# Low parts of the gate and value weights and the scaling of the output weights, on GpSimd instead of VectorE

## The chip, the cores and the metric

The kernel runs on one core of a Trainium2 chip. The metric is device time in microseconds (us). The core has five engines with a queue of instructions each: TensorE (PE; its weight loads are shown as PEld), VectorE (DVE), ScalarE (ACT), GpSimd (POOL) and SyncE (SP, which here issues DMAs). An engine takes its instructions in order; semaphores make it wait for others.

## The reference

Three layers, one after the other, in 32-bit floats (weights come as 64-bit words):

```python
scores = (q @ k.T) / sqrt(64)                  # 4 batches, 8 heads, 576 rows, 64 wide
attn = softmax(where(scores >= max(scores) - tau, scores, -1e9))
x = (attn @ v)  ->  2304 tokens x 512          # heads side by side
xn = x / rms(x) * rms_g                        # first MLP: 512 -> 1536 -> 512
g = xn @ w_gate
y = (silu(g) * (xn @ w_val)) @ w_out
P = exp(y @ gate - max); 8 x (rows and columns of P scaled)
out = sum over 8 experts e of P[:, e] * (relu(y @ w1[e]) @ w2[e])   # 512 -> 1024 -> 512
```

## The kernel before

A 32-bit operand goes through TensorE as two 16-bit parts: a high part (the value rounded) and a low part (the value minus the high part). A product is then three matmuls: high by high, high by low, low by high.

**Attention** runs over batches b, chunks c of 128 rows and heads h; a tile (b,c,h) is 128 x 576 scores. PE makes S (line 290), VectorE its maximum (300), ScalarE the exponent e (304), VectorE the mask (306), ScalarE the high part hl (311), GpSimd the low part in two pieces (312, 313), a transposing DMA makes eT (315), and PE multiplies with v into pv (338), three tiles behind S. After the eight heads of a chunk, `end_main` scales a row of tokens and makes xnT. Chunk 4 of a batch holds the 64 rows that are left and has four tiles of two heads.

**The first MLP** goes over nine pairs j of token blocks: `mlp_in(j)` makes gv (line 538) for 12 slices f of the hidden width, and `mlp_out(j)` 72 matmuls into x2 (572). The first pair needs the weights: `prep_group(gi)` calls `prep_in` for a third of the columns of the gate and of the value weights. There 64-bit words are loaded and turned into floats (lines 440 to 444) in the space of the output weights (`stage`, three places, the names `raw` and `wo`), a scale is found from their norms (465 to 470), ScalarE writes the high part (473), and the low part is made (474). `prep_out` converts the 12 slices of the output weights (also lines 440 to 444, with squares in line 498), finds a scale over all of them, and then for each slice scales it into one of two buffers r (515), makes the high part on ScalarE (516) and the low part on GpSimd (517).

The code is written in the order of the data, but a scheduler orders each engine's instructions by a timeline of its own, with attention given priority; so an operation on another engine moves others too, on all engines. Only the last stage, the experts, from about 790 us on, has an order of PE written out by hand (line 1148). This core of `prep_out` is what the change touches besides line 474:

```python
rr = pw.tile([P, 4, HD], F32, tag="x2", name="wof")
for f in range(KF):
    r = rr[:, f % 2 * 2 : f % 2 * 2 + 2].rearrange("p o d -> p (o d)")
    V.tensor_scalar(r, wo32[:, f], sf[:, f // n : f // n + 1], None, ALU.mult)
    A.activation(wo[:, f, 0, :], r, AF.Copy)
    G.tensor_tensor(wo[:, f, 1, :], r, wo[:, f, 0, :], ALU.subtract)
```

Of the kernel before, what the change touches and what calls it, by code (L numbers as in the profile page):

```python
# [12 lines left out]
ALU = mybir.AluOpType  # L13
# [6 lines left out]
def kernel(  # L20
# [24 lines left out]
    V, A, G, T = nc.vector, nc.scalar, nc.gpsimd, nc.tensor  # L45
# [371 lines left out]
    wo32 = wo.rearrange("p k l f -> p k (l f)").bitcast(F32)  # L417
# [33 lines left out]
    def prep_in(src, w, gi, name):  # L451

        bits = src.bitcast(I32)
        raw = stage[:, staged[0] % 3]
        staged[0] += 1
        ps = psx.tile([P, DM], F32, tag="mx", name=f"{name}n{gi}", bufs=1)
        cols = slice(gi * DM, (gi + 1) * DM)
        for kk in range(KD):
            wd = words(
                bits[kk * P : (kk + 1) * P, 2 * gi * DM : 2 * (gi + 1) * DM], f"{name}w{gi}_{kk}"  # L460
            )
            to_f32(raw[:, kk], wd, f"{name}l{gi}_{kk}")
            sq = pw.tile([P, 2 * P], F32, tag="u", name=f"{name}q{gi}_{kk}", bufs=2).bitcast(BF16)
            A.activation(sq, raw[:, kk], AF.Square)
            T.matmul(ps, lhsT=gsq[:, kk : kk + 1].to_broadcast([P, P]), rhs=sq, start=kk == 0, stop=kk == KD - 1)
        n2 = small([P, 1], name + "n2", bufs=2)
        V.tensor_reduce(n2, ps, AX.X, ALU.max)
        s, inv = norm_scale(n2, 1, 9, f"{name}{gi}")
        gs = small([P, KD], f"{name}gs{gi}")
        V.tensor_scalar(gs, g_sb, s[:, 0:1], None, ALU.mult)  # L470
        for kk in range(KD):
            sk, hi = gs[:, kk : kk + 1], w[:, 0, kk, cols]
            A.activation(hi, raw[:, kk], AF.Copy, scale=sk)
            V.scalar_tensor_tensor(w[:, 1, kk, cols], raw[:, kk], sk, hi, ALU.mult, ALU.subtract)
        return inv

    g32 = []
# [12 lines left out]
    def prep_out():  # L490

        bits = moe_w_out.bitcast(I32)
        n = KF // NG
        om = small([P, KF], "om")
        for f in range(KF):
            wd = words(bits[f * P : (f + 1) * P, :], f"wo{f}", ("x2", "x2t")[f % 2])
            sq = to_f32(wo32[:, f], wd, f"wol{f}").bitcast(BF16)[:, 0:DM]
            A.activation(sq, wo32[:, f], AF.Square, accum_out=om[:, f : f + 1])
        for _ in range(2):
            V.tensor_tensor(  # L500
                om.rearrange("p (g f) -> p g f", g=NG),
                om.rearrange("p (g f) -> p g f", g=NG),
                igv.to_broadcast([P, NG, n]),
                ALU.mult,
            )
        om1 = small([P, 1], "om1")
        V.tensor_reduce(om1, om, AX.X, ALU.max)
        s, inv = norm_scale(all_max(om1, "womx"), 1, 9, "wout")
        V.tensor_scalar(ixs, inv, 2.0**10, None, ALU.mult)
        sf = small([P, NG], "wosf")  # L510
        V.tensor_scalar(sf, igv, s[:, 0:1], None, ALU.mult)
        rr = pw.tile([P, 4, HD], F32, tag="x2", name="wof")
        for f in range(KF):
            r = rr[:, f % 2 * 2 : f % 2 * 2 + 2].rearrange("p o d -> p (o d)")
            V.tensor_scalar(r, wo32[:, f], sf[:, f // n : f // n + 1], None, ALU.mult)
            A.activation(wo[:, f, 0, :], r, AF.Copy)  # L516
            G.tensor_tensor(wo[:, f, 1, :], r, wo[:, f, 0, :], ALU.subtract)

# [163 lines left out]
    for t in range(len(row) + LAG):  # L682
        before = tc.cur_priority
        with attention_order():
            if t < len(row):
                b, c, heads, n, g = row[t]
# [461 lines left out]
    with tc.manual_schedule(engines={mybir.EngineType.PE}):  # L1148
        for k, (c, j) in enumerate(ahead):
            u, f = c // 2, c % 2  # L1150
# [85 lines left out]
```

## Time and profile before

| | |
|---|---|
| time, median of 3 runs | 2144.69 us (2141.03 to 2146.65) |
| the profiled execution's own time | 2142.97 us |
| its span, first to last instruction | 2141.2 us |
| busy in the span: PE | 1958.7 us (91%) |
| VectorE | 1628.3 us (76%) |
| ScalarE | 1307.4 us (61%) |
| GpSimd | 1358.6 us (63%) |

A share is a mean over stages with different limits: attention with the preparation of the weights first, then attention with the first MLP, then the experts. The span is some 2 us shorter than the execution's own time, which has the start and the end around it.

### The profile page before, as it was taken

What the parts mean: (1) busy time and instruction counts of PE and PEld (TensorE: products, weight loads), DVE (VectorE), ACT (ScalarE), POOL (GpSimd) and SP (SyncE); (2) the same over time, 40 slices, a digit from 0 to 9 for tenths busy, and PEclk for the clock granted to TensorE, in tenths of its full rate; (3) what the DMA queues carried; (4) which work ended last, traced back from release to release, by engine and by line L of the source; (5) the groups of instructions that cost most, each with busy time, mean ns of one, the idle gap of its engine ahead of it and who ended that gap; (6) DMA issues with size and microseconds to landing.
All of it is one profiled execution on the core that took longest, in us unless ns stands there. A gap on an engine that the chain in (4) does not pass through costs nothing.

```text
span 2141.2 us, 43769 instructions
## 1 busy us (share of the span) xinstructions
PE 1958.7 (91%) x16462; PEld 1454.1 (68%) x16462; DVE 1628.3 (76%) x3408; ACT 1307.4 (61%) x2804; POOL 1358.6 (63%) x1404
## 2 busy tenths in 40 slices
PE   1458788899999899899999999999999999999999
PEld 0236556677776667677777777777777777777777
DVE  6898677778753345897888888888888888888866
ACT  5887777878752247656655555555556555555552
POOL 1346546567652347666777777677777777777754
PEclk9769999999999999999999999999999999999999
DMA  9977679877854818244343334334434443433332
GB/s 269 209 170 151 137 138 163 178 133 144 143 90 128 191 55 227 94 136 124 118 141 121 120 124 136 118 116 141 123 118 134 125 124 124 143 119 121 104 99 81
DMA packets 373669, 290.46 MB, mean 136 GB/s; under 512 B 286160, under 2 KB 299600, under 8 KB 373456
## 3 DMA queue, kind: packets, MB, share of 16 engines
q1 hardware_dynamic: 372864, 287.64, 51.8%
q8 instruction: 129, 2.11, 0.4%
q14 instruction: 84, 0.69, 0.1%
q0 software_dynamic: 64, 0.00, 0.0%
q10 hardware_dynamic: 528, 0.02, 0.0%
HBM read 195.71 MB, written 21.23 MB: 101 GB/s over the span
## 4 chain that ended last, share of the span: by engine, by line
PE 64%; DVE 2%; DMA 2%; SPq 2%; ACT 0%; issue 0%; POOL 0%; DVEq 0%; ACTq 0%; POOLq 0%
PE P L1090 30%; PE X L1022 17%; PE Z L1022 12%; PE gv L538 3%; PE x L572 2%; SPq L833 1%; DMA xo<-x2d 1%; DVE w L733 1%; DMA xs<-x2d 1%; SPq L837 0%; DVE acc L1104 0%; DMA x2d<-xs 0%; DMA eT<-hl 0%; PE pv L338 0%; PE logits L875 0%
## 5 line engine op out<-in xcount | busy, mean ns | idle before, releaser
L1090 PE MATMUL P<-w,h 128*128 128x256 f16 x6048 | 768.6, 273 | 12.7 <-DVE w1mx L133 7.6
L1090 PEld LDWEIGHTS <-h 128*128 128x128 f16 x6048 | 591.9, 98 | 151.5 <-issue 16.2
L1022 PEld LDWEIGHTS <-w 128*128 128x128 f16 x4032 | 394.9, 98 | 194.1 <-issue 3.4
L1100 DVE SCALAR_TENSOR_TENSOR acc<-P,coef,acc 128x256 f32<-128x256 f32 x882 | 412.7, 477 | 100.8 <-PE P L1090 89.7
L1022 PE MATMUL X<-xo,w 128*128 128x384 f16 x2304 | 438.2, 327 | 1.3 <-ACT u2b L1042 0.9
L1022 PE MATMUL Z<-xo,w 128*128 128x384 f16 x1728 | 327.9, 326 | 0.0
L312 POOL TENSOR_TENSOR hl<-e,hl 128x512 f16<-128x512 f32 x144 | 173.9, 1207 | 210.4 <-ACT hl L311 136.1
L538 PE MATMUL gv<-xnT,wg 128*128 128x256 f16 x1296 | 171.7, 281 | 18.6 <-DVE u L548 17.6
L538 PE MATMUL gv<-xnT,wv 128*128 128x256 f16 x1296 | 169.1, 279 | 0.0
L538 PEld LDWEIGHTS <-wg 128*128 128x128 f16 x1296 | 127.6, 101 | 40.7 <-issue 21.1
L572 PE MATMUL x<-wo,tT 128*128 128x512 f16 x648 | 147.3, 382 | 6.8 <-ACT wo L516 3.7
L338 PE MATMUL pv<-vs,eT 128*128 128x64 f16 (+1 forms) x2240 | 102.2, 201 | 46.9 <-DMA eT<-hl 42.5
L338 PEld LDWEIGHTS <-eT 128*128 128x128 f16 (+1 forms) x2240 | 91.2, 106 | 76.9 <-DMA eT<-hl 61.2
L538 PEld LDWEIGHTS <-wv 128*128 128x128 f16 x1296 | 128.7, 100 | 18.1 <-issue 0.4
L300 DVE TENSOR_REDUCE nt<-S 128x1 f32<-128x576 f32 x144 | 107.1, 750 | 40.8 <-PE S L290 40.5
L306 DVE SCALAR_TENSOR_TENSOR e<-S,nt,e 128x576 f32<-128x576 f32 x144 | 116.5, 810 | 23.2 <-ACT e L304 22.8
L290 PE MATMUL S<-kT,qT 128*128 128x288 f16 (+1 forms) x320 | 65.6, 312 | 66.1 <-DVE e L306 35.6
L553 POOL TENSOR_TENSOR tT<-u,tT 128x256 f16<-128x256 f32 x108 | 74.9, 694 | 73.0 <-ACT tT L552 72.9
L572 PEld LDWEIGHTS <-tT 128*128 128x128 f16 x648 | 62.9, 98 | 81.6 <-issue 12.5
L304 ACT ACTIVATE e<-S,nt,c 128x576 f32<-128x576 f32 x144 | 117.5, 818 | 0.2 <-issue 0.2
L311 ACT ACTIVATE hl<-e 128x576 f16<-128x576 f32 x144 | 97.0, 676 | 24.9 <-DMA eT<-hl 13.7
L547 DVE SCALAR_TENSOR_TENSOR u<-u,gv 128x256 f32<-128x256 f32 x108 | 44.8, 415 | 73.7 <-ACT u L546 72.9
(2539 smaller groups left out, 3669.8 us busy)
## 6 DMA issues: line engine op xcount, KB each, us to landing
xo<-x2s SPq DMA_DIRECT2D x319, 384.0 KB, 3.1
w1r<-in_moe_w_dram SPq DMA_DIRECT2D x17, 1024.0 KB, 5.0
w2r<-in_moe_w_dram SPq DMA_DIRECT2D x17, 1024.0 KB, 6.6
x2s<-xo SPq DMA_DIRECT2D x17, 384.0 KB, 2.8
wgatew<-in_moe_w_gate_dram SPq DMA_DIRECT2D x12, 512.0 KB, 5.5
wo<-in_moe_w_out_dram SPq DMA_DIRECT2D x12, 512.0 KB, 4.1
wvalw<-in_moe_w_val_dram SPq DMA_DIRECT2D x12, 512.0 KB, 4.2
x2d<-xs SPq DMA_DIRECT2D x24, 256.0 KB, 2.6
```

The lines of the kernel that those rows point to most:

```text
L300: V.tensor_reduce(mx, sv, AX.XY, ALU.max)
L304: A.activation(ev, sv, AF.Exp, bias=nt[:, 0:1], scale=st["c2"][:, c : c + 1])
L306: V.scalar_tensor_tensor(ev, sv, nt[:, 1:2], ev, ALU.is_ge, ALU.mult, accum_out=sums[:, slot : slot + 1])
L311: A.activation(hl[:, 0:S], e, AF.Copy)
L312: G.tensor_tensor(hl[:, S + REM :], e[:, 0 : NCH * P], hl[:, 0 : NCH * P], ALU.subtract)
L338: T.matmul(o, lhsT=a, rhs=r, start=n == 0, stop=n == len(mm) - 1)
L538: T.matmul(gv[:, a, :], lhsT=w[:, l, kk, f * P : (f + 1) * P], rhs=xt[:, r * KD + kk, :], start=n == 0, stop=n == 3 * KD - 1,)
L553: G.tensor_tensor(t[:, 1, :], u, t[:, 0, :], ALU.subtract)
L572: T.matmul(ps, lhsT=tT[f][:, l, o : o + P], rhs=wo[:, f, r, :], start=n == 0, stop=n == 3 * KF - 1,)
L1022: T.matmul(ps, lhsT=w[:, a, l, kk, f * P : (f + 1) * P], rhs=xb[:, r * 2 + kk, :], start=n == 0 and j in (0, 1, 3), stop=n == 5, skip_grou ...
L1090: T.matmul(ps, lhsT=hs[u, ao, f][:, l, jj * P : (jj + 1) * P], rhs=w2[h][:, bo, r, f, :], start=n == 0 and j in (0, 1, 3), stop=n == 5, sk ...
L1100: main[True] = V.scalar_tensor_tensor(y, ps, coef[h][:, i : i + 1], y, ALU.mult, ALU.add)
```

## The change

```diff
@@ prep_in @@
             A.activation(hi, raw[:, kk], AF.Copy, scale=sk)
-            V.scalar_tensor_tensor(w[:, 1, kk, cols], raw[:, kk], sk, hi, ALU.mult, ALU.subtract)
+            G.tensor_scalar(raw[:, kk], raw[:, kk], sk, None, ALU.mult)
+            G.tensor_tensor(w[:, 1, kk, cols], raw[:, kk], hi, ALU.subtract)
@@ prep_out @@
-            V.tensor_scalar(r, wo32[:, f], sf[:, f // n : f // n + 1], None, ALU.mult)
+            G.tensor_scalar(r, wo32[:, f], sf[:, f // n : f // n + 1], None, ALU.mult)
```

The low part of a gate or value weight (24 of 128 x 512) was one operation of VectorE: raw times its scale, minus the high part. Now GpSimd scales raw in place, after ScalarE has read it, and then subtracts. The scaling of an output weight's slice (12 of 128 x 512) goes from VectorE to GpSimd as it is. Lines behind 474 have numbers greater by one in the changed kernel.

The scheduler's order changes with it. On GpSimd, at the first gate weights (wgategs is their scale, wg and wv the gate and value weights, hl the low parts of attention tiles), there stood in the kernel before:

```order
L312 TENSOR_TENSOR hl0_0_6_407<-e0_0_6_403,hl0_0_6_407 128x512
L313 TENSOR_TENSOR hl0_0_6_407<-e0_0_6_403,hl0_0_6_407 128x64
L312 TENSOR_TENSOR hl0_0_7_439<-e0_0_7_435,hl0_0_7_439 128x512
L313 TENSOR_TENSOR hl0_0_7_439<-e0_0_7_435,hl0_0_7_439 128x64
L312 TENSOR_TENSOR hl0_1_0_472<-e0_1_0_468,hl0_1_0_472 128x512
L313 TENSOR_TENSOR hl0_1_0_472<-e0_1_0_468,hl0_1_0_472 128x64
L312 TENSOR_TENSOR hl0_1_1_504<-e0_1_1_500,hl0_1_1_504 128x512
L313 TENSOR_TENSOR hl0_1_1_504<-e0_1_1_500,hl0_1_1_504 128x64
L312 TENSOR_TENSOR hl0_1_2_544<-e0_1_2_540,hl0_1_2_544 128x512
L313 TENSOR_TENSOR hl0_1_2_544<-e0_1_2_540,hl0_1_2_544 128x64
L358 TENSOR_TENSOR rs0_574<-ms0_572,mhalf_58 128x1
```

and in the changed one:

```order
L474 TENSOR_SCALAR wo_104<-wo_104,wgategs0_917 128x512 x4
L475 TENSOR_TENSOR wg_102<-wo_104,wg_102 128x512 x2
L312 TENSOR_TENSOR hl0_0_6_407<-e0_0_6_403,hl0_0_6_407 128x512
L313 TENSOR_TENSOR hl0_0_6_407<-e0_0_6_403,hl0_0_6_407 128x64
L475 TENSOR_TENSOR wg_102<-wo_104,wg_102 128x512 x2
L312 TENSOR_TENSOR hl0_0_7_439<-e0_0_7_435,hl0_0_7_439 128x512
L313 TENSOR_TENSOR hl0_0_7_439<-e0_0_7_435,hl0_0_7_439 128x64
L474 TENSOR_SCALAR wo_104<-wo_104,wvalgs0_981 128x512 x4
L312 TENSOR_TENSOR hl0_1_0_472<-e0_1_0_468,hl0_1_0_472 128x512
L313 TENSOR_TENSOR hl0_1_0_472<-e0_1_0_468,hl0_1_0_472 128x64
L475 TENSOR_TENSOR wv_103<-wo_104,wv_103 128x512 x3
```

So the scalings and subtractions of the weights stand between the low parts of attention tiles, the four scalings of a group mostly in one piece. On the whole 24 scalings and 21 subtractions stand ahead of the end of tile (0,2,3) there.

On PE, at the end of batch 0 (pv0_4 are the last products with v of batch 0, x2_0 and x2_1 the output products of the first MLP, line 572), there stood before:

```order
L338 MATMUL pv0_4_3075<-vs0_0_229,eT0_4_0_2435 64x64
L338 LDWEIGHTS eT0_4_0_2435
L338 MATMUL pv0_4_3075<-vs0_0_229,eT0_4_0_2435 64x64
L572 LDWEIGHTS tT0_0_1265
L572 MATMUL x2_0_1763<-wo_104,tT0_0_1265 128x512
L572 LDWEIGHTS tT0_0_1265
L572 MATMUL x2_1_1809<-wo_104,tT0_0_1265 128x512
L572 LDWEIGHTS tT0_0_1265
L572 MATMUL x2_0_1763<-wo_104,tT0_0_1265 128x512
```

and now, behind the last hidden slice gv0_11:

```order
L539 MATMUL gv0_11_1604<-xnT0_579,wv_103 128x256
L290 LDWEIGHTS qT1_0_2478
L290 MATMUL S1_0_0_3129<-kT1_0_2217,qT1_0_2478 128x288
L290 LDWEIGHTS qT1_0_2478
L290 MATMUL S1_0_1_3178<-kT1_0_2217,qT1_0_2478 128x288
L290 LDWEIGHTS qT1_0_2478
L290 MATMUL S1_0_0_3129<-kT1_0_2217,qT1_0_2478 128x288
L290 LDWEIGHTS qT1_0_2478
L290 MATMUL S1_0_1_3178<-kT1_0_2217,qT1_0_2478 128x288
L539 LDWEIGHTS wv_103
L539 MATMUL gv0_11_1604<-xnT0_579,wv_103 128x256
L539 LDWEIGHTS wv_103
```

Before, 62 of the 72 output products stand ahead of the first S of batch 1; now S of its first two tiles stands ahead of all 72, and the rest of the 72 stand among tiles up to (1,1,2).

On GpSimd, at the same place (wof is the scaled output weight, line 516 the moved scaling), there stands now:

```order
L516 TENSOR_SCALAR wof_1750<-wo_104,wosf_1748 128x512
L554 TENSOR_TENSOR tT0_8_1539<-u0_11_1629,tT0_8_1539 128x256
L516 TENSOR_SCALAR wof_1750<-wo_104,wosf_1748 128x512
L518 TENSOR_TENSOR wo_104<-wof_1750,wo_104 128x512
L312 TENSOR_TENSOR hl1_0_0_3141<-e1_0_0_3137,hl1_0_0_3141 128x512
L313 TENSOR_TENSOR hl1_0_0_3141<-e1_0_0_3137,hl1_0_0_3141 128x64
L516 TENSOR_SCALAR wof_1750<-wo_104,wosf_1748 128x512
L312 TENSOR_TENSOR hl1_0_1_3190<-e1_0_1_3186,hl1_0_1_3190 128x512
L313 TENSOR_TENSOR hl1_0_1_3190<-e1_0_1_3186,hl1_0_1_3190 128x64
L518 TENSOR_TENSOR wo_104<-wof_1750,wo_104 128x512
L516 TENSOR_SCALAR wof_1750<-wo_104,wosf_1748 128x512
L518 TENSOR_TENSOR wo_104<-wof_1750,wo_104 128x512
```

Before, the twelve subtractions of line 517 stood there in two runs of 2 and 10 with nothing of batch 1 between them; now scalings and subtractions stand among its first tiles, the last behind tile (1,0,5).

## Rows read from the trace of the kernel before

**Rows 1.** The page: busy tenths in 40 slices of 53.5 us.
```profile
PE   1458788899999899899999999999999999999999
...
DVE  6898677778753345897888888888888888888866
...
POOL 1346546567652347666777777677777777777754
```

**Rows 2.** The page: chain that ended last, by engine.
```profile
PE 64%; DVE 2%; DMA 2%; SPq 2%; ACT 0%; issue 0%; POOL 0%; DVEq 0%; ACTq 0%; POOLq 0%
```

**Rows 3.** Windows: busy us of each engine in four stretches.
```profile
core 0: us, PE busy (x) PEld busy (x) DVE busy (x) ACT busy (x) POOL busy (x), PEclk, DMA share, GB/s
67.90:143.80 75.90, 36.39 (x340) 22.00 (x339) 69.82 (x159) 63.59 (x131) 29.38 (x30) 0.63 0.79 183
143.80:237.03 93.23, 73.30 (x710) 51.02 (x708) 81.39 (x192) 71.54 (x167) 51.31 (x59) 0.92 0.68 142
240.00:420.00 180.00, 156.18 (x1681) 117.96 (x1681) 132.00 (x324) 142.65 (x330) 102.76 (x141) 0.96 0.81 155
420.00:640.00 220.00, 208.60 (x2376) 161.14 (x2375) 157.41 (x361) 163.30 (x376) 145.70 (x196) 1.00 0.74 133
```

**Rows 4.** Groups of VectorE by form, 67.9 to 143.8 us.
```profile
L474 DVE SCALAR_TENSOR_TENSOR wg<-wo,wgategs,wg 128x512 f16<-128x512 f32 x12 | 9.5, 819 | 0.0
L474 DVE SCALAR_TENSOR_TENSOR wv<-wo,wvalgs,wv 128x512 f16<-128x512 f32 x8 | 6.2, 780 | 0.0
```

**Rows 5.** Groups of GpSimd by form, 67.9 to 143.8 us.
```profile
L312 POOL TENSOR_TENSOR hl<-e,hl 128x512 f16<-128x512 f32 x14 | 19.4, 1382 | 42.0 <-ACT hl L311 29.0 <-issue 13.0
L313 POOL TENSOR_TENSOR hl<-e,hl 128x64 f16<-128x64 f32 x14 | 9.2, 655 | 0.0
```

**Rows 6.** Lines by source, whole span: durations ns min/median/max, first and last start.
```profile
L312 POOL TENSOR_TENSOR hl<-e,hl x144: 1143/1157/2405, 47.3 to 619.8; 128x512 f16<-128x512 f32 x144
...
L313 POOL TENSOR_TENSOR hl<-e,hl x144: 295/306/1552, 48.5 to 620.9; 128x64 f16<-128x64 f32 x144
```

**Rows 7.** Lines by source, whole span: two-input operations of equal shape.
```profile
L474 DVE SCALAR_TENSOR_TENSOR wg<-wo,wgategs,wg x12: 735/742/1634, 69.7 to 138.6; 128x512 f16<-128x512 f32 x12
...
L733 DVE SCALAR_TENSOR_TENSOR w<-w1s,w_s,w x48: 744/1203/1477, 754.0 to 1998.0; 128x512 f16<-128x512 f32 x48
...
L798 POOL TENSOR_TENSOR w1s<-w1r,w1s x16: 1266/1588/1710, 702.1 to 1980.3; 128x512 f32<-128x512 f32 x16
```

**Rows 8.** Timeline, ACT and GpSimd: start, us, engine, line, operation, idle before.
```profile
67.23 2.55 ACT L473 ACTIVATE wg<-wo,wgategs 128x512 f16<-128x512 f32 x4
...
141.97 1.16 POOL L312 TENSOR_TENSOR hl<-e,hl 128x512 f16<-128x512 f32 x1 [3.82 <-issue]
143.09 0.75 POOL L313 TENSOR_TENSOR hl<-e,hl 128x64 f16<-128x64 f32 x1
...
237.03 1.16 POOL L312 TENSOR_TENSOR hl<-e,hl 128x512 f16<-128x512 f32 x1 [8.07 <-issue]
```

**Rows 9.** Groups by form, 143.8 to 237.0 us: output weights and the last low parts.
```profile
L515 DVE TENSOR_SCALAR wof<-wo,wosf 128x512 f32<-128x512 f32 x12 | 8.0, 683 | 1.6 <-POOL wo L517 1.5
...
L444 DVE SCALAR_TENSOR_TENSOR wo<-wo,wol 128x512 int32<-128x512 int32 x10 | 7.2, 724 | 0.0
...
L443 DVE SCALAR_TENSOR_TENSOR wol<-wo,wol 128x512 int32<-128x512 int32 x9 | 7.0, 793 | 0.0
L498 ACT ACTIVATE wol<-wo 128x512 bf16<-128x512 f32 x10 | 6.2, 623 | 0.1
...
L441 DVE TENSOR_SCALAR wol<-wo 128x512 int32<-128x512 int32 x9 | 4.2, 467 | 4.9 <-DMA wo<-in_moe_w_out_dram 4.9
...
L474 DVE SCALAR_TENSOR_TENSOR wv<-wo,wvalgs,wv 128x512 f16<-128x512 f32 x4 | 3.0, 799 | 0.0
```

**Rows 10.** Timeline of PE, around the first two output products of the first MLP.
```profile
205.76 0.79 PE L572 MATMUL x<-wo,tT 128*128 128x512 f16 x2 [2.45 <-ACT wo L516]
...
293.26 4.48 PE L572 MATMUL x<-wo,tT 128*128 128x512 f16 x20
```

## Prediction

> **What bounds the kernel now.** I read the slices of the page first [rows 1]. PE is at nine tenths or more from about the ninth slice on; before that, in the first 200 us, VectorE is the fullest engine and GpSimd mostly half idle or less. The chain that ended last [rows 2] is PE for 64% of the span: the later stages are matmul after matmul. So an early delay is not hidden by what comes behind it, unless PE there has holes; the question is when PE gets its work, and how much is left over for the stages where PE is full.
>
> Then I cut the early part at two attention tiles, because the change reorders everything else around them [rows 3, 8]. The first scaled gate weight is made on ScalarE at 67.2 us, so GpSimd could start at about 67.9. Tile (0,2,3) (batch 0, chunk 2, head 3) is done on GpSimd at 143.09 + 0.75 = 143.8, and the first tile of batch 1, (1,0,0), starts there at 237.0. In the first stretch (75.9 us) VectorE works 69.8 us, that is 0.92 of it, ScalarE 63.6, PE 36.4, GpSimd 29.4. In the second (93.2 us) VectorE works 81.4 (0.87), PE 73.3, ScalarE 71.5, GpSimd 51.3. After that PE is the fullest: 156.2 of 180 us, then 208.6 of 220 [rows 3].
>
> **What the change takes off VectorE.** Twenty of the 24 low parts (line 474) lie in the first stretch, 9.5 + 6.2 = 15.7 us [rows 4]; the other four, 3.0 us, and the twelve scalings of the output weights, 8.0 us, lie in the second [rows 9]. Together 26.7 us on the engine that is fullest in both.
>
> **What it adds on GpSimd.** 24 scalings, 24 subtractions, 12 scalings of output weights. A subtraction has the form of line 312 (two inputs, 128x512 to 16 bits): 1.382 us in this stretch, 1.157 in the median of the whole run [rows 5, 6]. No row shows a one-input operation on GpSimd. Its far bounds are 0.31 us from below (line 313, which has an eighth of the columns [rows 6]) and 1.27 from above (line 798, two inputs and a 32-bit result, at its least [rows 7]). Between them I interpolate: the medians at 64 and 512 columns are 0.306 and 1.157 us, so a column costs 1.90 ns and the rest 0.184; with one input instead of two I halve the column's cost, 0.184 + 512 x 0.95 ns = 0.67 us [rows 6]. In this stretch line 312 takes 1.382 / 1.157 = 1.19 times its median [rows 5, 6], so I take 0.80. This is an estimate; 0.67 and 1.0 are its near bounds.
>
> **First term, the attention behind the low parts.** The order of GpSimd puts all 24 scalings and 21 of the subtractions ahead of the end of tile (0,2,3), among the same 14 tiles as before. Each tile costs 1.382 + 0.655 = 2.04 us [rows 5]. Sum: 24 x 0.80 + 21 x 1.382 + 14 x 2.04 = 19.2 + 29.0 + 28.5 = 76.7 us. GpSimd had 42 us of waiting in front of line 312 there [rows 5], 29.0 of it for ScalarE; now it becomes the fullest engine, and VectorE falls to 69.8 - 15.7 + 6.6 = 60.7 (the 6.6 is explained below). If the fullest engine again works 0.92 of the stretch, it lasts 76.7 / 0.92 = 83.4 us and ends at 151.3: **7.5 us later**. With 0.67 or 1.0 for the scaling it is 4.1 or 12.7 later. Queued behind each scaling are the subtractions of attention tiles; for them wait the transposing DMAs on SP's queue, and for these the pv products on PE.
>
> **Second term, the stretch behind it.** The order of VectorE now has 16 instead of 6 of the 36 conversions of output weights (lines 441 to 444) ahead of tile (0,2,3): 10 x (0.467 + 0.793 + 0.724) / 3 = 6.6 us have moved forward [rows 9]. So the second stretch loses 6.6 + 3.0 + 8.0 = 17.6 us of VectorE, which falls to 63.8. ScalarE loses the casts and squares of 3.3 conversions, some 6.6 x 0.62 = 4.1 us (the cast taken like the square [rows 9]), and is then the fullest with 67.4. At 0.87 of the stretch this is 77.2 instead of 93.2: **16.0 us less**. The bounds: 17.6, all of VectorE's relief, and 10, if GpSimd's queue, which now also holds the scalings, takes a good third of it back.
>
> **Third term, what PE has not done by then.** In before's order 62 of the 72 output products of the first MLP (line 572) stand ahead of S of tile (1,0,0); in after's order none does, as the pieces above show. Before, PE does them while it waits for the output weights (the first line of [rows 10]); now they come where PE is full. Twenty take 4.48 us at speed [rows 10], so 62 x 0.224 = **13.9 us** of PE work are carried over. The first products of the second MLP (gv1_0) stand behind tile (1,1,4) instead of (1,0,3); this changes which work fills PE, not how much, and I cost it at nothing: attention's products for these nine tiles then lie on PE earlier. If GpSimd can't feed nine tiles in a row, it costs some us more, which the range must hold.
>
> **Sum.** +7.5 - 16.0 + 13.9 = +5.4 us. Against the profiled execution (2142.97 us, 1.7 below the median of the three runs) this is 2148.4; against the median, 2144.69, it is 2150. I predict 2150 us. A measurement of this kernel can tell about 0.3%, 6.4 us, from no change; the forecast lies just inside that. With the near bounds of the first and second term it runs from 4.1 - 17.6 + 13.9 = +0.4 to 12.7 - 10 + 13.9 = +16.6, so 2145 to 2161.
>
> **Rival 1, which ends faster: the carried-over products cost nothing.** Between 240 and 420 us PE is without work for 180 - 156.2 = 23.8 us [rows 3]. If the 62 products fall into such holes, the third term is gone: 7.5 - 16.0 = -8.5, 2136 us. The point from which this decides: 11.8 of the 13.9 us must land in holes (13.9 - 11.8 leaves -6.4 in all). For it speaks that the products need only tT and the output weights, both there by then; against it, that these products stand in a fixed order among S and pv that wait themselves. If half of them fit, the sum is -1.6: no change.
>
> **Rival 2: GpSimd and VectorE hold each other up.** The rows show it here already: line 313 takes 0.306 us in the median of the run but 0.655 in the crowded stretch [rows 5, 6], and an operation of VectorE of the same shape as line 474 takes 1.203 in the median of line 733, late in the kernel where GpSimd is busy over seven tenths, against 0.742 [rows 1, 7]. If in the first stretch the scaling takes 1.0 and the subtraction 1.588, as the slowed line 798 does [rows 7], GpSimd needs 24.0 + 33.3 + 28.5 = 85.8 us, the stretch 93.3 and the first term is +17.4; if VectorE's relief in the second comes to half, -8, the sum is +23: 2168 us. The Trainium skill has a rule that speaks for this rival (Perfetto Trace Analysis, Optimizing Scalar/DVE Operations): GpSimd and VectorE share a read port of SBUF, so that moving operations between the two may not help. By that rule the relief of 26.7 us would mostly come back as longer operations; the trace agrees in kind, with the 0.655 against 0.306.
>
> **Rival 3: GpSimd is not the bound.** If it keeps its medians (24 x 0.67 + 21 x 1.157 + 14 x 1.463 = 60.9 us), ScalarE with 63.6 + 4.1 = 67.7 is the fullest, the stretch lasts 73.6, the first term is -2.3 and the sum -4.4: 2140 us. Against it speaks that the two engines slow each other even at today's load.
>
> **How the numbers follow.** The forecast gets 0.45 (slower by over 0.3% in 0.22, within in 0.23, since its range lies about evenly on both sides of 2151); rival 1 gets 0.22 (faster 0.18, within 0.04); rival 2 0.17 (slower 0.16, within 0.01); rival 3 0.16 (within 0.12, faster 0.04). That is faster 0.22, within 0.40, slower 0.38. Signs being mixed, the forecast's own range is 2145 to 2161; the range to hold eight in ten reaches to rival 1 and most of rival 2: 2134 to 2165.
>
> **What would show it.** In the changed profile: the scaling on GpSimd at 0.7 to 1.0 us; GpSimd busy nine tenths or more between 68 and 150 us, and VectorE clearly below today's 0.92; tile (0,2,3) done on GpSimd near 151, tile (1,0,0) starting near 229 (237.0 + 7.5 - 16.0); line 572 running after that, among tiles of batch 1. From 420 us on the same PE share as now, and the last stage (from the logits on) as long as now and only shifted. The prediction fails if the scaling costs over 1.2 us, if tile (1,0,0) does not come earlier than today, or if the later order, which differs up to the end of attention, wins or loses more than some 5 us by itself.

## The result and the profile after

The changed kernel takes 2174.68 us (median of 4 runs, 2172.02 to 2175.75), the kernel before 2142.86 beside it; the ratio is 1.0145, with an interval from 1.0125 to 1.0165. It is slower by 1.45%, some 31 us. The forecast was 2150, its range ended at 2165.

The profiled execution of the changed kernel has a span of 2173.9 us, 32.7 more than before. From its page come the busy times and the slices (tenths, 53.5 to 54.3 us each):

```profile
PE 1959.2 (90%) x16462; PEld 1453.8 (67%) x16462; DVE 1626.9 (75%) x3372; ACT 1310.7 (60%) x2804; POOL 1441.2 (66%) x1464
...
PE   1436879888999989999999999999999999999999
...
DVE  6888676777763344698878888888888888888866
...
POOL 1895866565662337576777777777777777777754
```

PE is busy for as long as before (1959.2 against 1958.7); what came is 32.2 us of idle time. Against [rows 1], GpSimd goes from 3 and 4 tenths to 8 and 9 in the second and third slice, and PE falls from 5 and 8 to 3 and 6 in the third and fourth. Windows of the changed kernel, the first, third and later ones as in [rows 3], the other two cut at its own tile (0,2,3):

```profile
core 0: us, PE busy (x) PEld busy (x) DVE busy (x) ACT busy (x) POOL busy (x), PEclk, DMA share, GB/s
67.90:143.80 75.90, 30.87 (x255) 17.47 (x253) 61.89 (x114) 54.92 (x108) 74.37 (x59) 0.59 0.64 147
67.90:167.20 99.30, 36.90 (x309) 21.31 (x308) 81.76 (x147) 71.48 (x147) 92.50 (x75) 0.57 0.62 149
143.80:237.03 93.23, 52.62 (x608) 41.97 (x609) 74.79 (x165) 68.20 (x159) 64.35 (x70) 0.74 0.67 142
167.20:256.97 89.77, 66.53 (x720) 50.87 (x719) 67.93 (x155) 64.21 (x147) 59.81 (x66) 0.83 0.71 143
...
420.00:640.00 220.00, 202.11 (x2248) 154.43 (x2248) 162.80 (x381) 168.69 (x390) 141.59 (x194) 0.98 0.73 136
```

Between 67.9 and 143.8 us GpSimd now works 74.4 of 75.9 us, where it worked 29.4. VectorE has lost 15.7 us of low parts there and yet falls only from 69.8 to 61.9. The groups of GpSimd from 67.9 to the end of tile (0,2,3) say what fills it (busy us, mean ns, idle before):

```profile
L474 POOL TENSOR_SCALAR wo<-wo,wvalgs 128x512 f32<-128x512 f32 x12 | 21.3, 1790 | 1.8 <-ACT wv L473 1.8
L474 POOL TENSOR_SCALAR wo<-wo,wgategs 128x512 f32<-128x512 f32 x12 | 20.6, 1728 | 1.5 <-ACT wg L473 1.5
L312 POOL TENSOR_TENSOR hl<-e,hl 128x512 f16<-128x512 f32 x14 | 18.7, 1335 | 4.4 <-ACT hl L311 4.4
L475 POOL TENSOR_TENSOR wg<-wo,wg 128x512 f16<-128x512 f32 x12 | 13.7, 1147 | 0.0
L475 POOL TENSOR_TENSOR wv<-wo,wv 128x512 f16<-128x512 f32 x10 | 13.4, 1347 | 0.0
L313 POOL TENSOR_TENSOR hl<-e,hl 128x64 f16<-128x64 f32 x14 | 6.5, 468 | 0.0
```

The scaling is the largest item, 41.9 us, and with 1.73 to 1.79 us it costs more than twice the 0.80 of the forecast. Ahead of attention's line 312 there were 42.0 us of waiting [rows 5]; now 4.4 are left, and 3.3 ahead of the scalings. The timeline of GpSimd gives the two landmarks (start, us):

```profile
166.68 0.48 POOL L313 TENSOR_TENSOR hl<-e,hl 128x64 f16<-128x64 f32 x1
...
256.97 1.16 POOL L312 TENSOR_TENSOR hl<-e,hl 128x512 f16<-128x512 f32 x1 [1.91 <-ACT hl L311]
```

| | before | forecast | after |
|---|---|---|---|
| tile (0,2,3) done on GpSimd, us | 143.8 | 151.3 | 167.2 |
| first term | | +7.5 | +23.3 |
| from there to the start of tile (1,0,0), us | 93.2 | 77.2 | 89.8 |
| second term | | -16.0 | -3.4 |
| from there to the end, us | 1904.2 | | 1916.9 |
| third term | | +13.9 | +12.7 |

So the forecast's first term is 16 us too small, and its second has 13 us too much relief. Two waits grew: that of PE for the transposed low parts, and in SP's queue (SPq) that of the loads of the weights' words (line 429) for VectorE's conversions (line 444). Waits in us (total, times, longest), changed kernel from 67.9 to 167.2 us:

```profile
PE pv L338 <- DMA eT<-hl: 28.0, 7, 7.6
SPq L429 <- DVE wo L444: 47.1, 12, 17.0
```

and the kernel before from 67.9 to 143.8 us:

```profile
PE pv L338 <- DMA eT<-hl: 15.9, 8, 4.1
SPq L429 <- DVE wo L444: 12.2, 4, 7.2
```

The forecast named GpSimd as what holds the transposing DMAs up. The longest of PE's waits has another path. Its tile is (0,1,6) (timelines of the changed kernel: start, us, engine, line):

```profile
132.97 0.75 POOL L313 TENSOR_TENSOR hl<-e,hl 128x64 f16<-128x64 f32 x1
142.55 1.30 DVE L444 SCALAR_TENSOR_TENSOR wo<-wo,wol 128x512 int32<-128x512 int32 x1
143.92 0.33 SPq L429 DMA_DIRECT2D wo<-in_moe_w_out_dram  x1
144.42 2.18 SPq L315 DMA_TRANSPOSE eT<-hl  x1
148.82 0.93 PE L338 MATMUL pv<-vs,eT 128*128 128x64 f16 x14 [7.60 <-DMA eT<-hl]
```

The low part was done on GpSimd at 133.7. Its transposing DMA started 10.7 us later, behind the load of an output weight that had waited 17.0 us for VectorE to end a conversion (line 444).

### The profile page after: what moved, and what is told of

Same layout as the page of the kernel before. It is cut to its first block, busy times and chain, and to the rows that moved or that the text cites. A ratio compares the mean times of both kernels' runs of the same rounds, so it can differ in the third digit from the quotient of the medians.

```text
span 2173.9 us, 43803 instructions
## 1 busy us (share of the span) xinstructions
PE 1959.2 (90%) x16462; PEld 1453.8 (67%) x16462; DVE 1626.9 (75%) x3372; ACT 1310.7 (60%) x2804; POOL 1441.2 (66%) x1464
## 4 chain that ended last, share of the span: by engine, by line
PE 65%; DVE 2%; SPq 2%; DMA 2%; issue 1%; POOL 0%; ACT 0%; DVEq 0%; ACTq 0%; POOLq 0%
PE P L1091 30%; PE X L1023 16%; PE Z L1023 12%; PE gv L539 4%; PE x L573 2%; SPq L834 1%; DMA xo<-x2d 1%; DVE w L734 1%; DMA xs<-x2d 0%; PE pv L338 0%; PE S L290 0%; SPq L838 0%; DVE acc L1105 0%; DMA x2d<-xs 0%; PE logits L876 0%
## 5 line engine op out<-in xcount | busy, mean ns | idle before, releaser
L1091 PE MATMUL P<-w,h 128*128 128x256 f16 x6048 | 769.1, 273 | 12.7 <-DVE w1mx L133 7.6
```

What stands on the lines that cost most here:

```text
L1091: T.matmul(ps, lhsT=hs[u, ao, f][:, l, jj * P : (jj + 1) * P], rhs=w2[h][:, bo, r, f, :], start=n == 0 and j in (0, 1, 3), stop=n == 5, sk ...
```

## The experiments

Three theories. **A**: the price of the scaling fills GpSimd, and attention's low parts wait in its queue. **B**: the changed order of the work does it, above all the output products that fall behind the first batch. **C**: GpSimd and VectorE hold each other up where both read SBUF, so VectorE's relief comes back as longer operations. SP's queue, seen above, has no experiment of its own. Ratios are against the kernel before, run beside each (2140.7 to 2142.5 us).

**Which part of the change.** The gate and value weights alone, and the output weights alone:

```diff
 # first kernel: line 516 back
-            G.tensor_scalar(r, wo32[:, f], sf[:, f // n : f // n + 1], None, ALU.mult)
+            V.tensor_scalar(r, wo32[:, f], sf[:, f // n : f // n + 1], None, ALU.mult)
 # second kernel: only line 516 changed, line 474 as before
```

> Only the low parts of the gate and value weights on GpSimd; the scaling of the output weights stays on VectorE. Theory A (the scaling on GpSimd costs 1.56 to 1.75 us, twice the estimate, so GpSimd is full from 68 to 167 us and the attention tiles in its queue come late): GpSimd's order up to tile (0,2,3) is the same as in the changed kernel, so that tile is done near 167 again, the first term stays +23; only 8 scalings ahead of tile (1,0,0), 12.5 us of GpSimd, go away. I expect 2162 to 2172 us. Theory B (the order does it: no output product of the first MLP ahead of batch 1): that is so here too, 2157 or more, and tile (0,2,3) could be anywhere. Theory C (VectorE's relief is given back because the two engines slow each other): the low parts' conversions on VectorE again near 1.05 us, as in the changed kernel. If the output weights were the cause, it would be near 2143.

> Only the scaling of the output weights on GpSimd; the gate and value weights as before. Theory A: the twelve scalings at 1.56 us are 18.7 us on GpSimd in a stretch where it works 51 of 93 us, so there is room; tile (0,2,3) at 143.8 as before, time 2143 to 2150 us. Theory B: 24 instead of 62 output products stand ahead of batch 1, so 38 x 0.224 = 8.5 us are carried over: about 2151. Theory C: little, since few operations of VectorE lie beside them.

Measured: 2163.21 us (1.0103, 1.0089 to 1.0117) and 2148.79 (1.0036, 1.0024 to 1.0049). The first part costs some 22 us, the second some 8, together the 31. With the first alone tile (0,2,3) is done at 166.1, as A says, but tile (1,0,0) starts at 262.0, 5 us later than in the changed kernel. With the second alone it is done at 143.5 and tile (1,0,0) starts even earlier, at 232.6; but the last output weight is ready at 257.7 instead of 229.0 us, and the second MLP starts late. The last subtraction of line 517 (GpSimd) and the first product of line 538 behind the output products (PE), in the kernel with the output weights alone:

```profile
256.51 1.16 POOL L517 TENSOR_TENSOR wo<-wof,wo 128x512 f16<-128x512 f32 x1
...
267.94 2.77 PE L538 MATMUL gv<-xnT,wg 128*128 128x256 f16 x12
```

and in the kernel before:

```profile
226.52 2.45 POOL L517 TENSOR_TENSOR wo<-wof,wo 128x512 f16<-128x512 f32 x2 [1.42 <-ACT wo L516]
...
239.97 2.03 PE L538 MATMUL gv<-xnT,wg 128*128 128x256 f16 x12
```

At the start of tile (1,0,0) 37 of the 72 output products are done there, and all 72 before. The 35 behind are 35 x 0.224 = 7.8 us, and from that landmark to the end it takes 7.7 us longer than before. That is B's mechanism, and here its size too; but A's range (2143 to 2150) holds the time as well, and with a cheaper product in GpSimd's queue the last weight is ready earlier again (further below).

**What the scaling costs by itself.** The kernel before with a list of operations ahead of it, on scratch; in the 12.5 us from 3.5 us on, which hold the first run of each, VectorE works 2.0 us.

```diff
+    for _ in range(3):
+        G.tensor_scalar(pf[:, 1024:1536], s0, mhalf, None, ALU.mult)            # 427
+        G.tensor_scalar(pf[:, 1024:1280], s0[:, 0:256], mhalf, None, ALU.mult)  # 428
+        G.tensor_scalar(pf[:, 1024:1088], s0[:, 0:64], mhalf, None, ALU.mult)   # 429
+        G.tensor_scalar(pf[:, 1024:1536], s0, -0.5, None, ALU.mult)             # 430
+        G.tensor_scalar(h0, s0, mhalf, None, ALU.mult)                          # 431
+        G.tensor_copy(pf[:, 1024:1536], s0)                                     # 432
+        G.tensor_tensor(pf[:, 1024:1536], s0, mhalf.to_broadcast([P, 512]), ALU.mult)  # 433
+        G.tensor_tensor(pf[:, 1024:1536], s0, s1, ALU.mult)                     # 434
```

> The kernel before with a list of operations of GpSimd ahead of everything, on scratch, three times each: what a one-input operation costs. If it goes by columns, the scaling with a scale per partition takes 1.56 us at 512 columns and about half of that at 256; a constant scale or a copy the same or less; the product of two inputs with the scale broadcast 1.03, with two full inputs about 1.15. If the cause is that the two engines held each other, the scaling falls clearly below 1.5 here, where VectorE does little.

GpSimd's timeline (start, us), each form's first run:

```profile
3.63 0.54 POOL L425 MEMSET wg<- 128x512 f32 x1
4.14 1.58 POOL L427 TENSOR_SCALAR wg<-wg,mhalf 128x512 f32<-128x512 f32 x1
...
7.25 0.94 POOL L428 TENSOR_SCALAR wg<-wg,mhalf 128x256 f32<-128x256 f32 x1
...
9.72 0.43 POOL L429 TENSOR_SCALAR wg<-wg,mhalf 128x64 f32<-128x64 f32 x1
...
11.67 1.48 POOL L430 TENSOR_SCALAR wg<-wg 128x512 f32<-128x512 f32 x1
13.21 0.61 POOL L432 COPY wg<-wg 128x512 f32<-128x512 f32 x1
13.91 1.04 POOL L433 TENSOR_TENSOR wg<-wg,mhalf 128x512 f32<-128x512 f32 x1
15.03 1.26 POOL L434 TENSOR_TENSOR wg<-wg 128x512 f32<-128x512 f32 x1
```

The price is the operation's own: 1.58 us with VectorE nearly idle, (1.58 - 0.94) / 256 = 2.5 ns a column. An operation with one input is the dearest of the list, and the copy, with one input too, is cheaper than every product; the same scaling written as a product with the scale broadcast takes 1.04. Theory C doesn't explain the 1.58; it can at most explain what comes on top in the kernel, where the mean is 1.73 to 1.79.

**A cheaper price, and half of the move.** The scaling as a product with the scale broadcast; and the scaling on VectorE with only the subtraction on GpSimd; both with the output weights as before.

```diff
-            G.tensor_scalar(raw[:, kk], raw[:, kk], sk, None, ALU.mult)
+            G.tensor_tensor(raw[:, kk], raw[:, kk], sk.to_broadcast([P, DM]), ALU.mult)
 # the other kernel
+            V.tensor_scalar(raw[:, kk], raw[:, kk], sk, None, ALU.mult)
```

> Both operations on GpSimd, but the scaling as a product of two inputs with the scale broadcast along the row; output weights on VectorE as before. GpSimd's order up to tile (0,2,3) is that of the changed kernel, and 54 output products stand ahead of batch 1 instead of none. Theory A: if the product costs 1.2 to 1.3 us instead of 1.75, the first term is some 24 x 0.5 = 12 us smaller, tile (0,2,3) near 155, and the time 2150 to 2158. Theory B: 54 of 62 products back, worth 12 us against the kernel with the gate and value weights alone, whatever the price. If the product costs as much as the scaling, then A and B differ: A keeps tile (0,2,3) at 167 and the time above 2160, B gives 2150.

> The low parts in two operations, but the scaling in place on VectorE and only the subtraction on GpSimd; output weights as before. Theory A: GpSimd gets 21 x 1.38 = 29 us ahead of tile (0,2,3), and had 42 us of waiting there, so it is not the bound; VectorE keeps nearly its work (a scaling of about 0.68 us for 0.80). Tile (0,2,3) within 3 us of 143.8, time 2138 to 2150 us. Theory B: all 72 output products stand ahead of batch 1, so nothing is carried over: 2140 or less. Theory C: VectorE's operations there get slower by the added 29 us of GpSimd, so tile (0,2,3) comes some 5 to 8 us later and the time is near 2150.

Measured: 2159.57 us (1.0080, 1.0066 to 1.0094) and 2152.81 (1.0055, 1.0043 to 1.0068). The scaling took 1.04 us in the median of the gate weights and 1.22 of the value weights, in the first stretch 1.13 and 1.25 in the mean instead of 1.72 and 1.90; so the scalings gave back 12 x (0.59 + 0.65) = 15 us. The subtractions of the gate weights (1.34 us for 1.15) and line 313 took longer, and up to tile (0,2,3) GpSimd is busy 82.1 us instead of 92.0. Yet the tile came only 4 us earlier (162.1) and the time fell by 3.6, with intervals that overlap: A's price alone does not rule. VectorE is busy 81.4 of these 94.2 us, nearly as full as GpSimd. B fails as well: all 72 products are done at the start of tile (1,0,0), and the 54 that stand ahead of batch 1 again in the order were worth 12 us by its account. With the subtraction alone on GpSimd, which is then 47.3 of 75.9 us busy, the time is still 12 us above before, and tile (0,2,3) comes at 150.6: near what C expected (2150, the tile 5 to 8 us later) and above A's range.

**Relief without load, load without relief.** In the first kernel the low parts of the gate and value weights are left out (set to zero once, at the start), in the second VectorE makes them and GpSimd makes them again; in a third GpSimd takes 64 of 512 columns, and the rest of the low parts is zero.

```diff
 # relief without load
-            V.scalar_tensor_tensor(w[:, 1, kk, cols], raw[:, kk], sk, hi, ALU.mult, ALU.subtract)
 # load without relief: V's line stays, and behind it
+            G.tensor_scalar(raw[:, kk], raw[:, kk], sk, None, ALU.mult)
+            G.tensor_tensor(w[:, 1, kk, cols], raw[:, kk], hi, ALU.subtract)
 # narrow
+            G.tensor_scalar(raw[:, kk, 0:64], raw[:, kk, 0:64], sk, None, ALU.mult)
+            G.tensor_tensor(w[:, 1, kk, gi * DM : gi * DM + 64], raw[:, kk, 0:64], hi[:, 0:64], ALU.subtract)
```

> The low parts of the gate and value weights are left out (they are zero, set once at the start), so VectorE is relieved of 24 operations and GpSimd gets nothing; output weights as before. The second term of the prediction says that VectorE's relief is worth some 16 us in all, of which about 11 with these 24 operations: then 2130 us or less, and tile (1,0,0) well ahead of 237. If VectorE's share of nine tenths was not what held this stretch, it is 2137 to 2143. Theory A (the scaling's price on GpSimd explains the loss) and theory C (the two engines slow each other) both let the relief count, since nothing is added on GpSimd.

> VectorE makes the low parts as before, and GpSimd scales in place and subtracts all the same, writing the same low parts again; output weights as before. The load without the relief. If the relief is worth what the second term says, this is some 11 us or more slower than the kernel with only the gate and value weights moved (2163): 2174 or more. If the relief is worth nothing because GpSimd's queue sets the end, it is within 4 us of 2163, tile (0,2,3) near 166 and the scaling again 1.56 us at its least. Theory C: VectorE's own fused operation, two inputs, goes from 0.80 to over 1.0 us beside GpSimd.

> As the kernel with only the gate and value weights moved, but both operations on GpSimd take 64 of 512 columns (the other columns of the low parts are zero): the same instructions and waits in GpSimd's queue at a small price, some 0.4 to 0.5 us for a pair instead of 2.9. 62 output products stand ahead of batch 1, as before. Theory A: GpSimd gets 11 us instead of 70, tile (0,2,3) at 144 or earlier, time as in the kernel with the low parts left out, 2143 or less. If the waits in the queue (an operation on weights at its head, attention behind it) cost by themselves, tile (0,2,3) is 3 us or more later than there. Theory C: VectorE's conversions are back near 0.75 us.

Measured: 2132.82 us (0.9954, 0.9938 to 0.9970), 2162.84 (1.0095, 1.0075 to 1.0115) and 2143.29 (1.0002, 0.9989 to 1.0014). Relieved of 24 operations and with nothing in exchange, the kernel gains 9 us, less than the 11 that the second term gives these 24, and tile (1,0,0) starts at 226.9. With the load, it takes the same whether VectorE is relieved (2163.21) or not (2162.84). That equality comes about late: relieved, tile (0,2,3) is done at 166.1 instead of 171.0 and tile (1,0,0) starts at 262.0 instead of 270.5, but from there to the end it takes 1900.9 instead of 1885.6 us. So the relief is worth 5 to 8 us up to there, and what comes behind gives it back. A narrow pair costs 0.9 us instead of 3.0, and with it the gain is gone, and tile (0,2,3) is done 3.4 us later than without any pair.

**A load that reads nothing.** VectorE keeps its work, and GpSimd writes zeros over the spent weights, or copies or scales them in place.

```diff
+            for _ in range(5):
+                G.memset(raw[:, kk], 0.0)          # five, six, three settings to zero
+                G.tensor_copy(raw[:, kk], raw[:, kk])   # four copies; one
+                G.tensor_scalar(raw[:, kk], raw[:, kk], 1.0, None, ALU.mult)  # two scalings; one
```

> The kernel before, and behind each low part that VectorE makes, GpSimd sets the spent raw weights to zero five times (0.54 us each in the list of prices, 2.7 us for the 2.9 of scaling and subtraction): about the same time in GpSimd's queue, but it reads nothing. Theory A (occupied queue): as the load without relief, 2158 to 2165 us, tile (0,2,3) near 165 to 171. Theory C (the two engines share a way into SBUF and hold each other up): VectorE's fused operation stays below 0.85 us, and the time lies well below, 2145 to 2152, since what costs is VectorE's slowing.

> As the load of five settings to zero behind each low part, but four copies of the spent weights onto themselves (0.61 us each in the list of prices, 2.45 us instead of 2.7): less time in GpSimd's queue, but each reads. VectorE keeps all its work. Theory A (occupied queue): no slower than the settings to zero, 2150 us or less, tile (0,2,3) at 145 or earlier. Theory C (the engines hold each other up at the read): slower than those, 2155 or more; VectorE's fused operation, two inputs, over 1.0 us, and tile (0,2,3) some 10 us later.

> Six settings to zero instead of five, 3.25 us behind each low part: the same time in GpSimd's queue as scaling and subtraction beside busy VectorE (1.88 + 1.37 in the load without relief). Theory A: 20 x 0.55 = 11 us more for GpSimd in the first stretch, which is then full: 2157 to 2163 us and tile (0,2,3) near 160, as with scaling and subtraction. Theory C: a few us more than with five, 2150 to 2154.

> The same again with two scalings by 1.0 in place (1.49 us each, 2.98 us), an operation that reads more slowly than a copy. Theory A: between five and six settings to zero, so between their times. Theory C: as the four copies or above, since it holds VectorE up at each read and for longer: 2157 or more.

> The kernel before, and one copy of the spent weights onto themselves on GpSimd behind each low part that VectorE makes (24 copies, 0.61 us each in the list of prices); VectorE keeps its work, and the weights are converted ahead of attention as far as with one scaling, 83 pieces up to tile (0,2,3). Theory A (time in GpSimd's queue): 15 to 19 us of GpSimd where 42 were free, time within 3 us of before, 2139 to 2145. Theory C (VectorE is held up at each read): 24 times up to 0.6 us more for VectorE, 2145 to 2150.

> The same with one scaling by 1.0 in place (1.49 us) in place of the copy, in nearly the same order on all engines: only the price differs. Theory A: 36 to 43 us of GpSimd, some 21 more than with the copy, at the slope of the narrow and the broadcast runs (some 0.45 us of time for each us of GpSimd) 8 to 10 us more than with the copy. Theory C: it reads as much as the copy but holds on for longer, so the same or somewhat more, and VectorE's operations beside it longer than beside the copy.

> Three settings to zero instead (1.64 us), as long as one scaling and without a read. Theory A: as with one scaling, within 3 us. Theory C: clearly less than with one scaling, within 3 us of before, and VectorE's two-input operations near 0.78 us.

| behind each low part, GpSimd | time, us | ratio | GpSimd busy, 67.9 to 143.8 | tile (0,2,3) done |
|---|---|---|---|---|
| three settings to zero | 2147.98 | 1.0024 (1.0013 to 1.0035) | 52.9 | 145.9 |
| five | 2150.05 | 1.0038 (1.0024 to 1.0051) | 66.2 | 145.0 |
| six | 2154.45 | 1.0061 (1.0048 to 1.0074) | 68.7 | 139.5 |
| one scaling | 2137.36 | 0.9973 (0.9961 to 0.9986) | 54.5 | 153.1 |
| one copy | 2154.39 | 1.0054 (1.0040 to 1.0068) | 41.6 | 150.7 |
| two scalings | 2178.41 | 1.0178 (1.0162 to 1.0194) | 65.3 | 178.6 |
| scaling, subtraction | 2162.84 | 1.0095 (1.0075 to 1.0115) | 71.8 | 171.0 |

(Four copies: 2205.91, 1.0301; of the conversions of lines 441 to 444 VectorE has done only 56 when tile (0,2,3) is done, and 78 with five settings to zero, so the order differs and the run tells nothing of copies alone.) With five and six settings to zero and with two scalings the times came as C expected or within 0.5 us of it (2145 to 2152, 2150 to 2154, 2157 or more), not as A did. One copy, one scaling and three settings to zero contradict both. Twenty-four useless scalings make the kernel faster by 0.3%, and 24 copies, at 0.99 us in the first stretch instead of 1.71 and in nearly the same order, make it slower by 0.5%. That is 17 us between two kernels that both only add work to GpSimd; A wanted the copy cheaper, C the two alike. None of it is there at tile (1,0,0), which starts at 247.8 with the scalings and 248.3 with the copies; from there to the end it takes 1887.8 and 1907.3 us. What is left is the later order, which the scheduler draws up anew for each kernel: B in a wider sense, argued and not tested with the order held. Differences of this size between single kernels can't be put down to one cause.

The rows also show where VectorE gets slower. Its low part, two inputs from SBUF, by source over the whole span (ns min/median/max), beside scaling and subtraction, beside five settings to zero, and beside one scaling:

```profile
L474 DVE SCALAR_TENSOR_TENSOR wg<-wo,wgategs,wg x12: 735/1000/1640, 69.3 to 136.9; 128x512 f16<-128x512 f32 x12
L474 DVE SCALAR_TENSOR_TENSOR wv<-wo,wvalgs,wv x12: 732/1083/1642, 82.8 to 155.2; 128x512 f16<-128x512 f32 x12
```

```profile
L474 DVE SCALAR_TENSOR_TENSOR wg<-wo,wgategs,wg x12: 739/747/1657, 70.6 to 147.0; 128x512 f16<-128x512 f32 x12
L474 DVE SCALAR_TENSOR_TENSOR wv<-wo,wvalgs,wv x12: 696/742/1221, 85.1 to 162.5; 128x512 f16<-128x512 f32 x12
```

```profile
L474 DVE SCALAR_TENSOR_TENSOR wg<-wo,wgategs,wg x12: 733/740/1094, 72.1 to 140.6; 128x512 f16<-128x512 f32 x12
L474 DVE SCALAR_TENSOR_TENSOR wv<-wo,wvalgs,wv x12: 734/740/1575, 89.1 to 156.5; 128x512 f16<-128x512 f32 x12
```

GpSimd is 71.8, 66.2 and 54.5 us busy there. Beside scaling and subtraction, which read, the median is longer by a third and more; beside writes it has its 742 of before [rows 7]. But a load that reads doesn't always show in it: beside one scaling it stays at 740, beside two it is 746 and 940. And the conversions get longer beside writes too: with five settings to zero line 441 of the gate weights takes 0.77 us in the mean instead of 0.42, and line 443 of the value weights 0.96 instead of 0.73 (67.9 to 143.8 us). So reads aren't all that lengthens VectorE's work.

**Versions that might beat both.** The scaling of the output weights on GpSimd as a broadcast product; on ScalarE; on ScalarE for every second slice.

```diff
+            G.tensor_tensor(r, wo32[:, f], sf[:, f // n : f // n + 1].to_broadcast([P, DM]), ALU.mult)
 # on ScalarE (in the third kernel for odd f)
+            A.activation(r, wo32[:, f], AF.Copy, scale=sf[:, f // n : f // n + 1])
```

> Only the scaling of the output weights on GpSimd, as a product with the scale broadcast (1.04 instead of 1.56 us). With the plain scaling there the last output weight was ready at 257.7 instead of 228.9 us and the second MLP began 28 us later, for 8 us of time. Theory A (price): 12 x 0.52 = 6.2 us less in GpSimd's chain, so the last weight near 250, and the time between, 2144 to 2147. If it is the alternation of three operations on two buffers and two engines, whatever the price: 2148 again.

> A try at a version that beats both: the scaling of the output weights on ScalarE, which is 0.77 busy there, instead of VectorE with 0.87; nothing new on GpSimd. If VectorE holds that stretch, 8 us of relief give 2 to 5 us: 2136 to 2140. If the chain per slice counts (scaling and high part now both on ScalarE), the weights are ready later and it is 2141 or more.

> As the one before, but every second slice is scaled on ScalarE and the others on VectorE. If VectorE's share holds the stretch: half the gain, 2138 to 2141. If the chain of the output weights counts: the weights ready no later than in the kernel before, and the time at or a little below 2141.

Measured: 2144.39 us (1.0012, 1.0002 to 1.0023), 2134.30 (0.9962, 0.9948 to 0.9976) and 2141.48 (1.0000, 0.9987 to 1.0012). With the broadcast product the last weight is ready at 241.1 instead of 257.7, and some 5 of the 8 us are gone, as A says of the price. ScalarE for all twelve beats the kernel before by 8 us, more than the 2 to 5 that were expected; half of it gains nothing, so the cause may again be the order and stays open.

## Why the prediction was wrong

**The price of the scaling** is the first step that failed. "Between them I interpolate", it said, and "with one input instead of two I halve the column's cost": 0.67, in a crowd 0.80 us. The list shows 2.5 ns a column instead of 0.95, and 1.58 us even with VectorE nearly idle; in the changed kernel the scaling took 1.73 to 1.79. The number of inputs does not tell the price: with one input the copy took 0.61 and the scaling 1.58, with two the product took 1.26. The far upper bound, 1.27 from a two-input operation, was no bound.

**The first term** was mis-sized by this; its mechanism, a full GpSimd that holds attention up, is borne out, but not as the only one. Its sum, 19.2 + 29.0 + 28.5 = 76.7 us, becomes by the rows above 41.9 for 24 scalings, 27.1 for the subtractions and 25.2 for 14 tiles; GpSimd's busy time in the stretch is 92.5 us (records overlap a little). It works 0.93 of it, where 0.92 was taken, so the stretch is 99.3 instead of 83.4 us: +23.3. What this doesn't account for is how little a lower price gave back (4 us of tile (0,2,3) for the broadcast product): with GpSimd no longer full, something else held the stretch nearly as long. The forecast put SP's queue at nothing but the delay by GpSimd, and there the loads of weights wait for VectorE's conversions with transposing DMAs behind them. Up to tile (0,2,3) these waits are 47.1 us in the changed kernel and still 35.3 with the broadcast product, 12.2 before. The five kernels whose tile (0,2,3) comes behind 160 us have 35 to 55 us of them, all others 11 to 23. Whether they cause the delay or go with it, no run here tests.

**The second term** assumed that VectorE is the fullest engine behind the stretch and that the stretch shrinks with its work, at 0.87. VectorE's work did fall there, from 81.4 to 67.9 us (63.8 was forecast), but the stretch lost only 3.4 us: VectorE works 0.76 of it, PE 0.74, ScalarE 0.72 and GpSimd 0.67, so no engine's busy time sets its length. This is the second step that failed; what holds the stretch stays open. The granted clock is lower there (0.83 for 0.92), but PE's 720 matmuls take 66.5 us and the 710 before took 73.3, so no added time of PE shows for it. Without any load the relief of the 24 low parts goes with a gain (9 us; 10 earlier at tile (1,0,0)), though that is within what the order moves by itself. In the first stretch part of the relief came back as longer operations. Rows of VectorE from 67.9 to 143.8 us, changed kernel first, then the kernel before:

```profile
L444 DVE SCALAR_TENSOR_TENSOR wo<-wvalw,wvall 128x512 int32<-128x512 int32 x8 | 8.6, 1079 | 0.1
L443 DVE SCALAR_TENSOR_TENSOR wvall<-wo,wvall 128x512 int32<-128x512 int32 x8 | 8.3, 1049 | 5.3 <-ACT wo L440 5.3
L306 DVE SCALAR_TENSOR_TENSOR e<-S,nt,e 128x576 f32<-128x576 f32 x10 | 8.1, 806 | 1.3 <-ACT e L304 1.3
...
L441 DVE TENSOR_SCALAR wgatel<-wgatew 128x512 int32<-128x512 int32 x4 | 4.1, 1023 | 0.0
...
L470 DVE TENSOR_SCALAR wvalgs<-g_sb,wval_s 128x4 f32<-128x4 f32 x2 | 3.3, 1626 | 0.0
```

```profile
L306 DVE SCALAR_TENSOR_TENSOR e<-S,nt,e 128x576 f32<-128x576 f32 x14 | 11.3, 804 | 0.0
...
L444 DVE SCALAR_TENSOR_TENSOR wo<-wvalw,wvall 128x512 int32<-128x512 int32 x8 | 5.9, 760 | 0.0
L443 DVE SCALAR_TENSOR_TENSOR wvall<-wo,wvall 128x512 int32<-128x512 int32 x8 | 5.7, 728 | 0.0
...
L441 DVE TENSOR_SCALAR wgatel<-wgatew 128x512 int32<-128x512 int32 x4 | 1.6, 416 | 0.0
...
L470 DVE TENSOR_SCALAR wvalgs<-g_sb,wval_s 128x4 f32<-128x4 f32 x3 | 0.8, 250 | 0.0
```

The conversions of the value weights (443, 444) take 0.32 us longer each, those of the gate weights (441) 0.6, and a scale of 128 x 4 numbers takes 1.63 instead of 0.25 us, as long as one scaling of GpSimd. Sixteen of the first, four of the second and two of the third are 5.1 + 2.4 + 2.8 = 10.3 us, against the 15.7 that were taken off. Line 306, whose first input is S, keeps its 0.80. So rival 2 named a real effect, but its own price for the scaling, 1.0 us, was as wrong as the forecast's. The Trainium skill (SBUF — State Buffer, Who interferes with whom) states it more sharply than the page cited in the prediction: a VectorE operation with two SBUF inputs contends with a GpSimd operation that reads SBUF, and not with one that only writes. The trace agrees for the low part, with the 1000 and 1083 against 747 and 742 ns above, though one scaling, which reads, left it at 740. How much of the 22 us of the gate and value weights is this, how much GpSimd's full queue and how much SP's, the runs don't settle: loads of similar length without reads cost 8 and 13 us, with reads 21 and 37, but the order scatters times by up to 17.

**The third term** came out near its size (+12.7 for 13.9) by luck, not by its count: at the start of tile (1,0,0) 38 of the 72 products are done and all 72 before, so 34, not 62, were carried over, 34 x 0.224 = 7.6 us. The order of PE says what stands behind S of that tile, not what PE has done when GpSimd gets to it. With the output weights alone the count explains the loss; here 5 us stay open, and with the gate and value weights alone 12 products are behind and yet the rest is 3.3 us shorter than before. With the load without relief none is behind, and the rest is 18.6 us shorter.

**Of the conditions named for a failure**, two came: a scaling over 1.2 us, and a tile (1,0,0) that does not come earlier. The third, a later order that moves the time by more than 5 us by itself, is borne out by other kernels (the scalings and copies above); in the changed kernel it isn't shown apart. From 420 us on the shares did not stay either: PE works 202.1 of the 220 us behind that, in the kernel before 208.6.

## What to carry to other kernels

Before moving work to an engine that has not run that operation in the trace, measure the operation there: a bound taken from another operation on that engine, even one with more inputs, is none, and here it made the first term too small by 16 us. An engine that stands half idle is not free for a move when another engine's stream (here attention's low parts) passes through its queue; add the new work to what it has in that very stretch, and if the sum comes near the stretch, expect the move to cost what it overflows. Look at the DMA queue in the same way: what stands in it ahead of the transfer that counts may wait for a third engine. And where a scheduler redraws the order with each edit, calibrate with edits that should do little: here 24 useless scalings moved the time by -5 us and 24 useless copies by +13, so gains and losses of that size prove no cause.

## What was not expected of the hardware

In the list of prices, each on its first run, a 128x512 scaling on GpSimd with a scale per partition takes 1.58 us, with a constant 1.48, a copy 0.61, setting to zero 0.54, a product with a broadcast second input 1.04, and a product of two full inputs 1.26. A VectorE operation on 128 x 4 numbers (line 470, value weights) took 1.63 us in the mean of two beside GpSimd's scalings and 1.13 beside six settings to zero, for 0.25 before.
